# One row of W_down per partition, loaded from ScalarE's queue in transfers of 95 and 33 partitions

## The chip, the cores and the metric

The kernel runs on one core of one Trainium2 chip. The core has five engines that run side by side and wait for each other on semaphores: TensorE (PE in the profile) for matrix products, VectorE (DVE), ScalarE (ACT), GpSimd (POOL) and SyncE (SP). Data comes from the chip's memory into the on-chip buffer through 16 DMA engines. A load is issued by one of the engines into its own queue; the DMA engines then move it, packet by packet, and count a semaphore up as they finish. The metric is the time of one execution in device microseconds (us). Lower is better.

## The reference

One decode step, four sequences (B = 4), one token each, model width D = 576, in bfloat16:

```python
x = A_x
h = x + _A_ref(_layernorm(x), A_k_cache, A_v_cache, A_wq, A_wo)
h2 = h + _B_ref(_layernorm(h), B_W_gate, B_W_up, B_W_down)
```

`_A_ref` is attention with 32 query heads and 16 key/value heads of 128 over the last 4096 positions of a cache of 16384, with a softmax, followed by the product with `wo` (4096 x 576). `_B_ref` is a gated feed-forward layer:

```python
gate = x @ W_gate                    # 576 -> 4608
up   = x @ W_up                      # 576 -> 4608
h    = gate * (gate > 0) * up
return h @ W_down                    # 4608 -> 576
```

With one token per sequence nearly all of the work is reading: 159.6 MB of cache and weights are used once each.

## The kernel before

**Stages.** The kernel goes through `wq` and the queries, then through 16 groups of four key/value heads (each loads 4 MB of keys and 4 MB of values), then `wo`, then the gate and up products, then the product with W_down, and stores 4 x 576 values.

**Where loads land.** One large buffer, `pool`, has four slots of 4 MB. Keys and values go round these slots; `wo`, W_gate, W_up and W_down take the same space when its former users are done. `transfers` is the list of all loads in order, and SyncE issues them in that order (`prog_sync`), each after the instructions that last used its space.

**W_down.** It is laid out with 36 rows per partition: partition p holds rows 36p to 36p + 35, each of 576 values (1152 bytes), one after the other. `WD` at line 253 cuts the 36 rows of every partition into six pieces, (0, 14), (14, 23), (23, 29), (29, 33), (33, 35) and (35, 36), and each piece is one transfer of 128 partitions with its own semaphore (`wd0` to `wd5`). All six wait for "ATTN", the last product with `wo`, as they overwrite it. They are the last loads of the program.

**The end of the program, by engine.** ScalarE (`prog_act`, lines 345 to 358): after the attention it copies `oX`, takes the root for the second layer norm, copies the transposed activations (N1, N2), makes `hn4` in two activations (line 353, HN40 and HN41), then for each of three column ranges (`CUTS`) applies a relu to the gate product when PE has it (line 356), and at last casts the first 320 output columns. VectorE multiplies the up product by that (line 449), transposes the result in two halves (line 453, HHT 0 and 1), and casts the other output columns. PE (`prog_pe`) does the gate and up products (lines 573 to 592; each of the two is read in a part of four rows and a rest, with a semaphore each), and then, at lines 594 to 603, goes through the pieces of W_down in order: it waits for the piece's landing, and for the transposed half that it needs, and does two matmuls for each of the piece's rows.

**Names.** `S.op` and `S.dma` put an instruction on an engine's list, with the names that it waits for (`deps`) and the name under which others wait for it. `land(name)` is the name of a transfer's landing. On each engine the instructions run in the order in which they were put there. All matmuls are recorded at lines 466 and 468 of a helper, so the profile shows them under these lines and under the names of their tiles: `val<-pool,probT` at the end of the program is the product with W_down.

Of the kernel before, what the change touches and what calls it, by code (L numbers as in the profile page):

```python
# [12 lines left out]
D = 576  # L13
# [24 lines left out]
JJ = 36  # L38
# [63 lines left out]
def bass_sequential_preLN__sliding_block_cached__glu_gated_reglu__decode_kernel(  # L102
# [12 lines left out]
    with ExitStack() as es:  # L115
        cnt = [0]

        def sb(name, shape, dt):
            return es.enter_context(nc.sbuf_tensor(name, shape, dt))

        pool = sb("pool", [128, NSLOT * QUAD], BF16)
# [66 lines left out]
        def part(u, k, order):  # L188
            f0, f1 = CUTS[k]
            return pb[GUB[u][k]][:, 0:(f1 - f0) * JJ].rearrange("p (f j) -> p " + order, j=JJ)  # L190

        def down(u):
            n0, n1 = OUTS[u]
            return pb[DNB][32 * u:32 * u + B, 0:n1 - n0]
        tpv = pb[TPB].bitcast(BF16)

        S = Sched()
# [3 lines left out]
        transfers = []  # L201
# [49 lines left out]

        wd_sb = pool[:, 0:FC * D].rearrange("p (j n) -> p j n", j=JJ)
        WD = [(0, 14), (14, 23), (23, 29), (29, 33), (33, 35), (35, 36)]
        for k, (f0, f1) in enumerate(WD):
            transfers.append((("wd", k), f"wd{k}", ["ATTN"],
                              lambda e, f0=f0, f1=f1: e.dma_start(
                                  out=pool[:, f0 * D:f1 * D], in_=B_W_down.rearrange("(p j) n -> p (j n)", j=JJ)[:, f0 * D:f1 * D])))

        def feat(c):
            return slice(c, c + 509, 4) if c < 4 else slice(512, D)  # L260
# [1 line left out]
        def land(name):  # L262
            return ("L",) + (name if isinstance(name, tuple) else (name,))
# [25 lines left out]
        def prog_act(S):  # L289
# [3 lines left out]
                 deps=["D_VAR", "EPS"], name="A_STD")  # L293
            S.op(a, lambda e: e.copy(out=dup[:, :].rearrange("p (r u) -> p r u", u=2),
                                     in_=bass.AP(tensor=ident_b, offset=0, ap=[[128, 64], [1, 64], [0, 2]])), deps=["IDB"], name="DUP")
            S.op(a, lambda e: e.copy(out=col[:, :].rearrange("p (a s) -> p a s", s=NS),
                                     in_=bass.AP(tensor=ident_b, offset=0, ap=[[128, NS], [0, 128], [1, NS]])), name="COL")
# [3 lines left out]
                                           in_=bass.AP(tensor=ident_b, offset=0, ap=[[128, NS], [0, 16], [1, NS], [0, 2]]),  # L301
# [4 lines left out]
                                     in_=bass.AP(tensor=mask, offset=0, ap=[[NHQ, 128], [0, 16], [1, NHQ]])), deps=["M0"], name="SAME")  # L306
            for u in range(2):
                S.op(a, lambda e, u=u: e.activation(out=xn4[:, u, 0:B], in_=pb[STB][:, 0:B], func=ACT.Copy, scale=par[:, u:u + 1]),
                     deps=["XDUP", "PAR2", "XN4Z"], name=f"XN4{u}")
            for k in range(2):  # L310
                S.op(a, lambda e, k=k: e.copy(out=q_bf[:, k, :].rearrange("p (x e k) -> p x e k", e=2, k=32),
                                              in_=pb[QB[k]].rearrange("p (x k e) -> p x e k", e=2, k=32)), deps=["QMM"], name=f"QBF{k}")
            S.op(a, lambda e: e.copy(out=qrep[:, :, :].rearrange("p x (g y) -> p x g y", g=4),
                                     in_=sc.ap().rearrange("p (g r) -> p g r", g=4)[:, :, 0:128].rearrange("p g (x y) -> p x g y", x=4)),
                 deps=["QREP"], name="D_QR")
# [16 lines left out]
            for i in range(NQUAD):  # L332
                S.op(a, lambda e, i=i: e.activation(out=diag[:, i % 2, :], in_=spot[:, :], func=ACT.Copy, scale=rmx[:, i % 2:i % 2 + 1]),  # L333
                     deps=[("RMAX", i), "SPOT"], name=("DIAG", i))
                deps = [("BIAS", i)]
                if i >= 2:
                    deps.append(("TRP", i - 2))
                S.op(a, lambda e, i=i: e.activation(  # L338
                    out=Pb[:, (i % 2) * 1024:(i % 2 + 1) * 1024], in_=sc[:, (i % 2) * 1024:(i % 2 + 1) * 1024], func=ACT.Exp,
                    scale=SCALE, bias=bias[:, i % 2:i % 2 + 1], accum_out=rs1[:, i:i + 1]),  # L340
                    deps=deps, name=("EXP", i))
                if i + 2 < NQUAD:
                    qzero(i + 2)
            S.op(a, lambda e: e.copy(out=bass.AP(tensor=spread, offset=0, ap=[[16 * H, H], [4 * H + 1, 4], [4, H]]),
                                     in_=bass.AP(tensor=ident_b, offset=0, ap=[[128, H], [0, 4], [1, H]])),
                 deps=["SP0"], name="SPREAD")
            S.op(a, lambda e: e.copy(out=oX[:, :, :].rearrange("p e b -> p (e b)"), in_=pb[0][:, 0:EO * B]), deps=["OSEL"], name="OX")  # L347
            S.op(a, lambda e: e.activation(out=st2[:, 14:15], in_=st2[:, 13:14], func=ACT.Sqrt, bias=eps_c[0:B, 0:1], scale=1.0),
                 deps=["D_VAR2"], name="A_STD2")
            S.op(a, lambda e: e.copy(out=hnT[0:64, 4, 0:B], in_=tpv[0:64, 16:20]), deps=["TP2", "HN4Z"], name="N1")  # L350
            S.op(a, lambda e: e.copy(out=hnT[:, 0:4, 0:B], in_=tpv[:, 0:16].rearrange("p (c b) -> p c b", b=B)), name="N2")
            for u in range(2):
                S.op(a, lambda e, u=u: e.activation(out=hn4[:, u, 0:B], in_=pb[SUB][:, 400:400 + B], func=ACT.Copy, scale=par[:, u:u + 1]),
                     deps=["HDUP"], name=f"HN4{u}")
            for k, (f0, f1) in enumerate(CUTS):
                S.op(a, lambda e, k=k, f0=f0, f1=f1: e.activation(out=gate_sb[:, :, f0:f1].rearrange("p j f -> p f j"), in_=part(0, k, "f j"), func=ACT.Relu),
                     deps=[("GATE", k)], name=("RELU", k))
# [101 lines left out]
        def prog_pe(S):  # L459
            t = "tensor"  # L460

            def mm(o, l, r, start, stop, deps=(), name=None, skip=False, held=False):

                def make(e):
                    if not held:
                        return e.matmul(o, lhsT=l, rhs=r, start=start, stop=stop, skip_group_check=skip)  # L466
                    tile = tuple(next(x for x in (32, 64, 128) if x >= n) for n in (l.shape[0], l.shape[-1]))
                    return e.add_instruction(mybir.InstMatmult(  # L468
                        name=nc.get_next_instruction_name(), start_tensor_calc=start, stop_tensor_calc=stop, bass_skip_group_check=skip,
                        tile_size=tile, tile_position=(0, o.offset // o.ap[0][0] % 128), ldweights=False,  # L470
                        ins=[e.lower_ap(r), e.lower_ap(l)], outs=[e.lower_ap(o)]))

                S.op(t, make, deps=deps, name=name, signal=name is not None)
# [9 lines left out]
            for c in (4, 0, 1, 2, 3):  # L483
                s = at[("wq", 0)] + c * HQ if c < 4 else at[("wq", 4)]
                deps = [land(("wq", 0)), "D_XNT"] if c == 0 else [land(("wq", 4)), "XN41"] if c == 4 else []
                for g in range(4):
                    x0 = s + (g if c < 4 else g % 2) * 1024
                    for k in range(2):
                        mm(pb[QB[k]][32 * g:32 * g + 32, :], xnT[:, c, :] if c < 4 else xn4[:, g // 2, :], pool[:, x0 + 512 * k:x0 + 512 * k + 512], c == 4, c == 3,
                           deps=deps, name="QMM" if c == 3 and g == 3 and k == 1 else None, skip=True, held=k == 1)  # L490
                        deps = []
            for g in range(4):
                mm(pb[g][:, 0:128].rearrange("p (x h b) -> p x h b", x=4, b=B), sel[32 * g:32 * g + 32, :, :].rearrange("p g k -> p (g k)"),
                   qT[32 * g:32 * g + 32, :].rearrange("p (h x b) -> p x h b", x=4, b=32)[:, :, :, 0:B], True, True,
                   deps=["D_QT", "SEL"] if g == 0 else [], name="QREP" if g == 3 else None)
# [42 lines left out]
            for i in range(NQUAD + VLEAD):  # L538
# [5 lines left out]
                if i >= VLEAD:  # L544
                    j = i - VLEAD
# [7 lines left out]
            for q in range(4):  # L553
                mm(pb[0][:, 0:EO * B], spread[:, q, :, :].rearrange("p h k -> p (h k)"), o_bf[:, q * EO:(q + 1) * EO, :].rearrange("p e b -> p (e b)"), q == 0, q == 3,
                   deps=["NORM", "SPREAD"] if q == 0 else [], name="OSEL" if q == 3 else None)
            for e_ in range(EO):
                deps = [land(("wo",)), "OX"] if e_ == 0 else []
                for u in range(2):
                    c0 = at[("wo",)] + e_ * D + u * HD
                    mm(attn[:, u * HD:(u + 1) * HD], oX[:, e_, :], pool[:, c0:c0 + HD], e_ == 0, e_ == EO - 1,  # L560
                       deps=deps, name="ATTN" if e_ == EO - 1 and u == 1 else None, held=u == 1)
                    deps = []
# [10 lines left out]
            for u, kind in ((0, "wg"), (1, "wu")):  # L573
                if u == 1:
                    residual()
                for c in range(4):
                    s = at[(kind, 0)] + c * F
                    deps = [land((kind, 0))] + (["N2"] if c == 0 and u == 0 else [])
                    for k, (f0, f1) in enumerate(CUTS):
                        for q in range(4):  # L580
# [3 lines left out]
                            deps = []  # L584
                s = at[(kind, 4)]
                deps = [land((kind, 4)), "HN41"]
                for k, (f0, f1) in enumerate(CUTS):
                    for q in range(4):
                        x0 = s + (q % 2) * FQ
                        mm(pb[GUB[u][k]][32 * q:32 * q + 32, 0:(f1 - f0) * JJ], hn4[:, q // 2, :], pool[:, x0 + f0 * JJ:x0 + f1 * JJ],  # L590
                           False, True, deps=deps, name=(("GATE", "GU")[u], k) if q == 3 else None, skip=True, held=k > 0)
                        deps = []

            for k, (f0, f1) in enumerate(WD):
                deps = [land(("wd", k))]
                for f in range(f0, f1):
                    if f % (JJ // 2) == 0:
                        deps = deps + [("HHT", f // (JJ // 2))]
                    for u in range(2):
                        last = f == FC - 1  # L600
                        mm(down(u), hhT[:, f, 0:B], wd_sb[:, f, OUTS[u][0]:OUTS[u][1]], False, last,
                           deps=deps, name="DOWN1" if last and u == 1 else None, skip=True)
                        deps = []

        progs = [("gpsimd", prog_pool), ("sync", prog_sync), ("scalar", prog_act), ("vector", prog_dve), ("tensor", prog_pe)]
        S.begin(False)
        for _, p in progs:
# [32 lines left out]
```

## Time and profile before

| what | value |
|---|---|
| median of 3 runs | 377.72 us (377.6 to 378.23) |
| the profiled execution | 378.56 us, of which the span from first to last instruction is 377.2 us |
| read from memory | 159.58 MB, 423 GB/s over the span |
| SyncE's queue (q1) | 6488 packets, 98.8% of 16 engines' span |
| instruction loads (q8) | 8 packets, 0.13 MB |
| the six W_down transfers | 2016, 1296, 864, 576, 288 and 144 KB; 15.0, 17.7, 19.3, 20.2, 20.4 and 20.3 us from issue to landing |
| mean granted TensorE clock | 0.923 |

How to read it: times are counted from the start of the span. In the timeline a line gives the start, the duration, the engine, the line of the kernel, the operation, what it writes and reads, how many instructions were merged, and in square brackets how long the engine was idle before and what ended that. PEld is PE's loading of weights. In tables by stretch of time, the columns are the stretch, its length, the busy time and number of instructions of PE, PEld, DVE, ACT and POOL, the granted clock, the mean busy share of the 16 DMA engines, and GB/s; a packet is counted where it starts, so a share can come out a little over 1. Section 3 of the page gives for each queue its packets, megabytes and the time that its packets took as a share of all 16 engines. The trace doesn't say which of the 16 engines moved a packet.

### The profile page before, as it was taken

Reading aid. Unit: us, or ns where it says so; the run is one execution under the profiler, and the core shown is the slowest. Engines: PE = TensorE matmul, PEld = TensorE weight load, DVE = VectorE, ACT = ScalarE, POOL = GpSimd, SP = SyncE. Lnnn points to the kernel's source line nnn. Section 1 sums busy time; section 2 is a strip of 40 time slices with the busy share of each in tenths; the row PEclk is TensorE's granted clock in tenths of the full one; section 3 lists DMA queues with packets and bytes.
Section 4 is the critical chain, followed back from the end, with each engine's and each line's share of the span. In section 5 each row is a group of like instructions: output and inputs, shape, how many; then the busy total and the mean of one; then the engine's idle time right before and its main releaser. Section 6 shows DMA issues by size and latency. Waiting matters only on the chain.

```text
span 377.2 us, 2603 instructions
## 1 busy us (share of the span) xinstructions
PE 302.2 (80%) x1432; PEld 73.0 (19%) x772; DVE 225.8 (60%) x165; ACT 53.4 (14%) x140; POOL 5.2 (1%) x15
## 2 busy tenths in 40 slices
PE   0509299969996999499969996899879996968667
PEld 0101022212221222022212221122112121212214
DVE  8046677595849493858476846666675768231230
ACT  2202402110220112002200220020202010101020
POOL 5000000000000000000000000000000000000000
PEclk9999789998999899989989997799959998996988
DMA  8999999999999999999999999999999999999996
GB/s 334 445 445 389 445 440 393 445 440 438 422 424 441 438 434 408 441 441 427 413 440 441 431 427 427 440 434 427 420 441 440 417 424 441 422 432 429 443 404 255
DMA packets 6506, 159.74 MB, mean 423 GB/s; under 512 B 728, under 2 KB 864, under 8 KB 1632
## 3 DMA queue, kind: packets, MB, share of 16 engines
q1 hardware_dynamic: 6488, 159.59, 98.8%
q8 instruction: 8, 0.13, 0.1%
q10 hardware_dynamic: 8, 0.00, 0.0%
q14 instruction: 2, 0.02, 0.0%
HBM read 159.58 MB, written 0.00 MB: 423 GB/s over the span
## 4 chain that ended last, share of the span: by engine, by line
DMA 47%; DVE 29%; PE 20%; ACT 3%; SPq 1%; issue 1%; DVEq 0%
DMA pool<-in_A_k_cache_dram 41%; DVE kT L403 20%; PE sc L466 7%; PE sc L468 6%; DMA pool<-in_B_W_down_dram 5%; DVE acc L420 4%; PE val L466 3%; PE val L468 3%; DVE own_sb L417 2%; DVE probT L414 2%; ACT P L338 2%; PE pb L466 1%; DVE o_bf L442 0%; ACT L338 0%; DVE rmx L406 0%
## 5 line engine op out<-in xcount | busy, mean ns | idle before, releaser
L403 DVE STREAM_TRANSPOSE kT<-pool 128x2048 f32<-128x2048 f32 x64 | 142.8, 2278 | 25.3 <-DMA pool<-in_A_k_cache_dram 24.3
L466 PE MATMUL sc<-kT,qz 128*128 128x512 bf16 x256 | 110.5, 432 | 36.6 <-DVE kT L403 36.3
L468 PE MATMUL sc<-kT,qz 128*128 128x512 bf16 x256 | 109.6, 428 | 0.0
L466 PE MATMUL val<-pool,probT 128*64 128x512 bf16 (+2 forms) x328 | 104.2, 374 | 4.4 <-DMA pool<-in_B_W_down_dram 4.4
L468 PE MATMUL val<-pool,probT 128*64 128x512 bf16 x256 | 96.2, 379 | 0.0
L466 PEld LDWEIGHTS sc<-kT,qz 128*128 128x128 bf16 x256 | 26.7, 104 | 146.5 <-issue 71.1
L466 PEld LDWEIGHTS val<-pool,probT 128*64 128x64 bf16 (+1 forms) x328 | 32.1, 107 | 81.3 <-issue 68.5
L406 DVE TENSOR_REDUCE rmx<-sc 128x1 f32<-128x1024 f32 x16 | 19.6, 1225 | 41.0 <-PE sc L468 41.0
L333 ACT ACTIVATE diag<-spot,rmx 128x16 f32<-128x16 f32 x16 | 4.9, 307 | 234.0 <-DVE rmx L406 234.0
L414 DVE STREAM_TRANSPOSE probT<-P 128x1024 bf16<-128x1024 bf16 x16 | 19.9, 1246 | 21.0 <-ACT P L338 21.0
L338 ACT ACTIVATE P<-sc,bias 128x1024 bf16<-128x1024 f32 x16 | 17.8, 1114 | 21.0 <-DVE bias L409 21.0
L327 ACT COPY qz<-qrep 32x128 bf16<-32x128 bf16 x64 | 18.8, 294 | 0.6
L409 DVE TENSOR_REDUCE bias<-pb 128x1 f32<-128x16 f32 x16 | 2.8, 175 | 23.8 <-PE pb L466 23.8
L420 DVE TENSOR_REDUCE acc<-own_sb 128x128 f32<-128x1024 f32 x8 | 15.2, 1897 | 0.3
L417 DVE TENSOR_TENSOR own_sb<-val,mask 128x1024 f32<-128x1024 f32 x8 | 9.6, 1200 | 7.9 <-PE val L468 7.9
L466 PE MATMUL sc<-pool,oX 128*4 128x288 bf16 x32 | 10.0, 338 | 0.4 <-ACT oX L347 0.4
L468 PE MATMUL sc<-pool,oX 128*4 128x288 bf16 x32 | 9.9, 336 | 0.0
L478 PE MATMUL pb<-ident_b,xn_bf 4*128 4x4 bf16 (+1 forms) x5 | 0.4, 180 | 10.0 <-DVE xn_bf L371 10.0
L466 PE MATMUL sc<-qT,sel 32*128 32x128 bf16 x4 | 0.3, 284 | 9.6 <-DVE qT L427 9.6
L445 DVE TENSOR_TENSOR h_row<-sc,x_bf 4x576 f32<-4x576 f32 x1 | 0.7, 745 | 11.6 <-PE sc L468 11.6
L466 PE MATMUL pb<-diag,same 128*128 128x16 f32 x32 | 6.3, 273 | 1.7 <-ACT diag L333 1.7
L466 PEld LDWEIGHTS pb<-diag,same 128*128 128x128 f32 x32 | 4.8, 188 | 11.8 <-ACT diag L333 7.4
(102 smaller groups left out, 85.7 us busy)
## 6 DMA issues: line engine op xcount, KB each, us to landing
pool<-in_A_k_cache_dram SPq DMA_DIRECT2D x16, 4096.0 KB, 26.8
pool<-in_A_v_cache_dram SPq DMA_DIRECT2D x16, 4096.0 KB, 26.4
pool<-in_A_wo_dram SPq DMA_DIRECT2D x1, 4608.0 KB, 18.3
pool<-in_B_W_gate_dram SPq DMA_DIRECT2D x1, 4608.0 KB, 18.6
pool<-in_B_W_up_dram SPq DMA_DIRECT2D x1, 4608.0 KB, 24.7
pool<-in_A_wq_dram SPq DMA_DIRECT2D x1, 4096.0 KB, 12.7
pool<-in_B_W_down_dram SPq DMA_DIRECT2D x1, 2016.0 KB, 15.0
pool<-in_B_W_down_dram SPq DMA_DIRECT2D x1, 1296.0 KB, 17.7
```

The lines of the kernel that those rows point to most:

```text
L327: S.op(a, lambda e, src=src, dst=dst: e.copy(out=dst, in_=src), deps=deps, name=("QZ", i) if g == 3 else None, signal=g == 3)
L333: S.op(a, lambda e, i=i: e.activation(out=diag[:, i % 2, :], in_=spot[:, :], func=ACT.Copy, scale=rmx[:, i % 2:i % 2 + 1]), deps=[("RMAX", ...
L338: S.op(a, lambda e, i=i: e.activation(out=Pb[:, (i % 2) * 1024:(i % 2 + 1) * 1024], in_=sc[:, (i % 2) * 1024:(i % 2 + 1) * 1024], func=ACT ...
L403: S.op(v, lambda e: e.transpose(out=dst, in_=src), deps=deps, name=("TR", f))
L406: S.op(v, lambda e: e.tensor_reduce(out=rmx[:, i % 2:i % 2 + 1], in_=sc[:, (i % 2) * 1024:(i % 2 + 1) * 1024], axis=AX.X, op=ALU.max), dep ...
L409: S.op(v, lambda e: e.tensor_reduce(out=bias[:, i % 2:i % 2 + 1], in_=pb[TPB][:, 16 * (i % 2):16 * (i % 2) + 16], axis=AX.X, op=ALU.min), ...
L414: S.op(v, lambda e: e.transpose(out=pT[i % NPT], in_=Pb[:, (i % 2) * 1024:(i % 2 + 1) * 1024]), deps=[("EXP", i)] + ([("PV", i - NPT)] if ...
L417: S.op(v, lambda e: e.tensor_tensor(out=own_sb[:, :].rearrange("p (x d) -> p x d", d=DH), in0=val[:, :].rearrange("p (x d) -> p x d", d=DH ...
L420: S.op(v, lambda e: e.tensor_reduce(out=acc[:, w % 2, :], in_=own_sb[:, :].rearrange("p (x d) -> p d x", d=DH), axis=AX.X, op=ALU.add), de ...
L445: S.op(v, lambda e: e.tensor_tensor(out=h_row[:, :], in0=attn, in1=x_bf[:, :], op=ALU.add), deps=["ATTN", land("x")], name="H")
L466: return e.matmul(o, lhsT=l, rhs=r, start=start, stop=stop, skip_group_check=skip)
L468: return e.add_instruction(mybir.InstMatmult(name=nc.get_next_instruction_name(), start_tensor_calc=start, stop_tensor_calc=stop, bass_ski ...
```

## The change

Row 28 of every partition, the last of piece 2, is left out of SyncE's third W_down transfer, which so has 5 rows per partition in place of 6. It is loaded by two further transfers, one for partitions 0 to 94 and one for partitions 95 to 127. ScalarE issues them, behind the `hn4` activations and in front of the first gate activation; they wait for ATTN, and they share one semaphore, `wdrow`, whose full count is named by the second. PE waits for that count, besides `wd2`, in front of piece 2. The bytes loaded, the place where they land and all arithmetic are the same.

```diff
         WD = [(0, 14), (14, 23), (23, 29), (29, 33), (33, 35), (35, 36)]
+        wd_src = B_W_down.rearrange("(p j) n -> p (j n)", j=JJ)
+
+        def piece(f0, f1, p0=0, p1=128):
+            return lambda e: e.dma_start(out=pool[p0:p1, f0 * D:f1 * D], in_=wd_src[p0:p1, f0 * D:f1 * D])
+
         for k, (f0, f1) in enumerate(WD):
-            transfers.append((("wd", k), f"wd{k}", ["ATTN"],
-                              lambda e, f0=f0, f1=f1: e.dma_start(
-                                  out=pool[:, f0 * D:f1 * D], in_=B_W_down.rearrange("(p j) n -> p (j n)", j=JJ)[:, f0 * D:f1 * D])))
+            transfers.append((("wd", k), f"wd{k}", ["ATTN"], piece(f0, f1 - (k == 2))))
...
                      deps=["HDUP"], name=f"HN4{u}")
+            for p0, p1 in ((0, 95), (95, 128)):
+                S.dma("scalar", piece(28, 29, p0, p1), "wdrow", deps=["ATTN"], name=land("wdrow") if p0 else None)
             for k, (f0, f1) in enumerate(CUTS):
...
             for k, (f0, f1) in enumerate(WD):
-                deps = [land(("wd", k))]
+                deps = [land(("wd", k))] + ([land("wdrow")] if k == 2 else [])
                 for f in range(f0, f1):
```

## The prediction

> **What bounds the kernel now.** I read the page first: how much the transfers fill the span, and what closes the chain.
>
> ```profile
> span 377.2 us, 2603 instructions
> PE 302.2 (80%) x1432; PEld 73.0 (19%) x772; DVE 225.8 (60%) x165; ACT 53.4 (14%) x140; POOL 5.2 (1%) x15
> DMA packets 6506, 159.74 MB, mean 423 GB/s; under 512 B 728, under 2 KB 864, under 8 KB 1632
> q1 hardware_dynamic: 6488, 159.59, 98.8%
> q8 instruction: 8, 0.13, 0.1%
> q10 hardware_dynamic: 8, 0.00, 0.0%
> ```
>
> SyncE's queue (q1) keeps the 16 DMA engines busy for 98.8% of the span. Nothing on PE, DVE or ACT can shorten that; only fewer bytes, a shorter start or a shorter end can. So I read the end: the chain of waits in order of time, then the timeline of PE and ACT.
>
> ```profile
> 353.78 20.18 DMA pool<-in_B_W_down_dram
> 374.00 0.70 PE val L466 x7
> 374.72 0.68 PE val L466 x5
> 375.42 0.42 DVE out_sb L456
> ```
> ```profile
> 356.32 0.42 ACT L353 ACTIVATE hn<-val,par 128x4 bf16<-128x4 f32 x2 [0.20 <-PE val L466]
> 359.76 1.51 ACT L356 ACTIVATE P<-sc 128x396 f32<-128x396 f32 x2 [3.02 <-PE sc L466]
> 361.07 0.10 PEld L466 LDWEIGHTS pb<-pool,hnT 128*32 128x32 bf16 x4 [0.71 <-DMA pool<-in_B_W_up_dram]
> 367.48 4.95 PE L466 MATMUL val<-pool,probT 128*4 128x320 bf16 x46 [3.77 <-DMA pool<-in_B_W_down_dram]
> 372.63 0.98 PE L466 MATMUL val<-pool,probT 128*4 128x320 bf16 x12 [0.21 <-DMA pool<-in_B_W_down_dram]
> 375.07 0.08 PEld L466 LDWEIGHTS val<-pool,probT 128*4 128x4 bf16 x2 [0.27 <-DMA pool<-in_B_W_down_dram]
> ```
>
> From 353.78 on the end is set by W_down's landings: PE waits before the pieces wd0, wd2, wd3, wd4 and wd5, and behind the last landing only two matmuls, two casts and the store are left. So the last engine's last row is the end. Do the 16 engines stop together? Short windows of the tail show it (the last two columns are the DMA share and GB/s):
>
> ```profile
> 372.40:372.80 0.40, 0.19 (x5) 0.15 (x6) 0.00 (x0) 0.00 (x0) 0.00 (x0) 1.00 1.03 400
> 373.00:373.20 0.20, 0.20 (x9) 0.18 (x4) 0.00 (x0) 0.00 (x0) 0.00 (x0) 1.00 0.61 242
> 373.60:373.80 0.20, 0.01 (x1) 0.00 (x0) 0.00 (x0) 0.00 (x0) 0.00 (x0) 1.00 0.51 202
> 374.00:374.20 0.20, 0.20 (x4) 0.17 (x6) 0.00 (x0) 0.00 (x0) 0.00 (x0) 1.00 0.51 184
> 374.40:374.60 0.20, 0.20 (x5) 0.00 (x0) 0.00 (x0) 0.00 (x0) 0.00 (x0) 1.00 0.08 29
> ```
>
> They don't. Between 372.8 and 373.1 the share falls from 1.03 to 0.61: six engines have stopped. It holds at 0.51, eight engines, until 374.2, and at 374.5 about one is left (0.08). So eight engines run some 1.5 us behind the best, and one of them a further 0.2 to 0.3 us. The page fits: eight instruction loads of 16 KB (q8: 8 packets, 0.13 MB), each about 1 us on one engine, and eight late engines. The trace doesn't number the engines, and this is what the prediction turns on.
>
> **The change, part by part.** The sum is made against the profiled execution, 378.56 us with a span of 377.2; the median of the runs is 377.72, and I add the difference to the median.
>
> *ScalarE issues two transfers in front of gate's activations.* The one issue on ScalarE, x's, took 554 ns, so two take 1.1 us. They stand behind the hn activations (done at 356.74) and in front of the first gate activation, which waits 3.02 us for PE until 359.76. They end near 357.9: 1.9 us of cover. Were it gone, the gate activations, DVE's products and its transposes would slip by at most 1.1 us; the transposes end at 366.4 and PE waits for wd0 until 367.48, so that too would cost almost nothing. The wait on ATTN ends at 352.4, before ScalarE gets there. Cost 0.
>
> *SyncE keeps its 45 loads.* The third piece of W_down has 5 rows per partition in place of 6; an issue there is the same instruction. Cost 0.
>
> *PE waits for one more landing, wdrow, in front of piece 2.* Queued behind it are 26 matmuls, the casts and the store. PE reaches that point at 372.43, some 14.5 us after the second issue. SyncE's transfers issued at 352 to 355 took 15.0 to 20.4 us to land because they queue behind each other; the new rows stand in ScalarE's queue. If that queue takes turns row by row, each engine has about 26 SyncE rows to serve before wd1 is in (2 of W_up's long ones, then 8 each of three transfers) against at most 22 new ones, so wdrow lands in time. Cost 0; what it costs if not is in rival two.
>
> *The same bytes on other engines.* Each 128-row load makes 128 data packets and 16 completions (45 x 144 + 8 = 6488 in q1); x with 4 rows makes 4 and 4 (q10: 8). So 128 rows go as 8 to each of 16 engines, 4 rows as 1 to each of 4: equal shares. Equal shares of 95 = 5 x 19 on at most 16 engines are 19 rows on 5; of 33 = 3 x 11, 3 rows on 11. The other end is an even spread, about 8 rows each, which changes nothing. I take equal shares, since both rows of the trace have them. [...]
>
> *Price of a row.* With all engines busy (369.0 to 369.6: 438 GB/s at a share of 1.038) an engine moves 422 / 16 = 26.4 bytes per ns. Between 374.10 and 374.25, 24 packets, 22 of them of 1152 B, kept 54.5% of 16 engines busy: 1.308 us, less two of 2304 B at 87 ns, is 52 ns each. Between 374.0 and 374.7, 28.0% for 54 such rows, 3 of 2304 B and 11 completions leaves 6 ns for a completion. Inside a longer row, 1152 B cost 44 ns, so taking row 28 out of piece 2 saves each engine 8 x 44 = 350 ns. Then:
> - engines in the five: 19 x 52 + 6 - 350 = +640 ns, and +810 ns if they also take 3 of the 33;
> - engines with 3 rows only: 3 x 52 + 6 - 350 = -190 ns;
> - engines with none: -350 ns.
>
> *Rows that alternate with another queue's.* Not in this trace for such rows. Below: the two 8 KB loads of q14 at 78 us took 1.5% of 16 x 2.5 us, 0.3 us each, which is their bytes at 26.4 B/ns: nothing extra. Above: a 16 KB load of q8 took 1.5% of 16 x 4 us = 0.96 us at 56 us and 1.12 us at 360, against 0.62 by bytes: 0.34 to 0.50 extra for one change of queue. A gain is excluded, as the engines are full. I take nothing extra (8 KB is nearer to 1152 B) and keep the other end for the range.
>
> *The sum.* The end moves with the latest engine. If at least one of the five is among the eight late ones, the end is that engine's: +0.64 to +0.81 if it is the very last, 0.25 less if it is one of the other seven: +0.4 to +0.8, and I take 0.65. If all five are early, the latest lose 0.19 to 0.35: that much gain. Which? Five fixed engines miss eight late ones only if the eight lie in the other eleven: 4 of 16 placings if the eight are neighbours on a ring, 165 of 12870 if they are scattered. So the likelier is a loss: 377.72 + 0.65 = 378.4 us.
>
> **The rivals.**
> *One: the five are the early ones.* Six engines stop by 373.1, so five with 1.5 us to spare exist; with +0.81 they end near 373.9, still before the others. The end comes 0.19 to 0.35 earlier, 377.4 to 377.5; PE's own work allows it (it is free at 372.43, 373.61 and before each later piece). Against it: the placing count above. It is the case on the other side of no change.
>
> *Two: a change of queue costs.* At 0.42 us each, once per transfer: 2 x 0.42 + 0.81 = +1.65, 379.4. Once per row on the five: 22 x 0.42 + 0.81 = +10.05, 387.8, and PE would then wait for wdrow itself. From some 5 ns per row on it lifts the forecast over the 0.2% line. For it: all eight q8 loads go with late engines. Against: q14's two.
>
> *Three: spread evenly.* Then the same rows run on the same engines at 52 in place of 44 ns: 8 x 8 ns = +0.06 us, 377.8. [...]
>
> **How the numbers follow.** 0.2% is 0.755 us, about what a measurement of this kernel can tell from no change. Forecast (late engines loaded): 0.40; its prices run from +0.4 to +0.8 with nothing added for the change of queue and a few ns per row carry it over the line, so I put 0.22 of it above and 0.18 within. Queue change: 0.30, slower. Early five: 0.18, within. Even: 0.07, within. Something that gains more than 0.755, as engines lagging less for a reason not seen: 0.05. Together slower 0.52, same 0.43, faster 0.05. The range reaches down to 377.3 (early five) and up to 380.5, past one change per transfer; it leaves out the per-row end (about 0.10) and the larger gain. The forecast's own range is 378.1 to 378.7.
>
> **What would show it.** Equal shares: q10 with 8 + 128 + 5 + 11 = 152 packets; evenly spread, 8 + 128 + 32 = 168. Right: a tail in which fewer engines work longer, with a DMA share near 0.31 (five engines) or less after 374.6, and PE's last wait ending at 375.5 to 375.9 in place of 375.07. Early five: the plateau at 0.51 ends 0.2 to 0.35 sooner and PE's last wait ends at 374.7 to 374.9. Queue change: q10's share above its 128 x 52 ns = 6.7 us (0.1% of 16 engines' span), or PE's wait in front of piece 2 grown. ScalarE's first gate activation moved would show the issue not covered. I am wrong if the last landing doesn't move, or if a PE wait other than W_down's takes the end.

## The result, and the profile after

| | median (us) | executions | lowest to highest |
|---|---|---|---|
| before | 377.75 | 17 | 377.56 to 378.42 |
| after | 378.57 | 17 | 378.15 to 379.1 |

After over before is 1.0019, 95% interval [1.0013, 1.0026]: 0.8 us slower. The forecast was 378.4 us, in the range 377.3 to 380.5. The total came out near it. The way to the total did not.

The two profiled executions have nearly the same time (378.56 before, 378.61 after; spans 377.2 and 377.3), so their spans must not be compared directly: in the profiled execution of after, the loads ahead of the change, which it doesn't touch, ran about 0.8 us earlier. I take a mark ahead of the change, the packet with which the first DMA engine completes the last part of W_gate. From there to the last completion of W_down it was 347.87 to 374.69 before, 26.82 us, and 347.06 to 374.69 after, 27.63 us. The tail is 0.81 us longer, as the medians are.

The page of after, its span and its DMA lines (queue: packets, MB, share of 16 engines' span):

```profile
span 377.3 us, 2606 instructions
DMA packets 6650, 159.74 MB, mean 423 GB/s; under 512 B 744, under 2 KB 1008, under 8 KB 1776
q1 hardware_dynamic: 6488, 159.44, 98.7%
q8 instruction: 8, 0.13, 0.1%
q10 hardware_dynamic: 152, 0.15, 0.1%
```

q10 has 152 packets: 8 for x, 128 rows, and 5 + 11 completions. That is the equal-shares case; an even spread would have made 168.

The end of the chain of waits of after, in order of time (start, duration, what; its pieces of 0.02 to 0.04 us called "issue" are left out):

```profile
351.01 23.00 DMA pool<-in_B_W_down_dram
374.05 0.71 PE val L471 x7
374.77 0.66 PE val L471 x5
375.46 0.42 DVE out_sb L461
```

It is the same chain as before: W_down's landings set the end, and behind them only the last matmuls and the casts are left. The timeline of after, for ScalarE's first gate activation and for PE's waits:

```profile
357.43 1.49 ACT L361 ACTIVATE P<-sc 128x396 f32<-128x396 f32 x2 [3.45 <-PE sc L471]
360.71 0.11 PEld L471 LDWEIGHTS pb<-pool,hnT 128*32 128x32 bf16 x4 [3.00 <-DMA pool<-in_B_W_up_dram]
367.77 4.56 PE L471 MATMUL val<-pool,probT 128*4 128x320 bf16 x46 [3.05 <-DMA pool<-in_B_W_down_dram]
372.67 0.98 PE L471 MATMUL val<-pool,probT 128*4 128x320 bf16 x12 [0.33 <-DMA pool<-in_B_W_down_dram]
374.05 1.36 PE L471 MATMUL val<-pool,probT 128*4 128x320 bf16 x14 [0.41 <-DMA pool<-in_B_W_down_dram]
375.11 0.08 PEld L471 LDWEIGHTS val<-pool,probT 128*4 128x4 bf16 x2 [0.25 <-DMA pool<-in_B_W_down_dram]
```

The gate activation waited for PE, 3.45 us, and not for the two issues ahead of it. No wait in front of piece 2 takes the end: the last of the new rows was complete at 368.9, two us ahead of piece 1. PE's last wait ends at 375.11, against 375.07 before; counted from the mark that is 28.05 us against 27.20. So the last landing did move, by about 0.85 us, a little past the 0.43 to 0.83 that the prediction named as its sign.

The short windows of the tail of after (the last two columns are the DMA share and GB/s):

```profile
372.40:372.80 0.40, 0.13 (x3) 0.11 (x5) 0.00 (x0) 0.00 (x0) 0.00 (x0) 1.00 0.92 369
373.00:373.20 0.20, 0.20 (x7) 0.19 (x4) 0.00 (x0) 0.00 (x0) 0.00 (x0) 1.00 0.72 271
373.60:373.80 0.20, 0.04 (x1) 0.00 (x0) 0.00 (x0) 0.00 (x0) 0.00 (x0) 1.00 0.64 248
374.00:374.20 0.20, 0.15 (x4) 0.13 (x6) 0.00 (x0) 0.00 (x0) 0.00 (x0) 1.00 0.55 196
374.40:374.60 0.20, 0.20 (x6) 0.01 (x1) 0.00 (x0) 0.00 (x0) 0.00 (x0) 1.00 0.10 35
```

The staircase is still there. But these windows stand at the times of before's page, and after's loads run 0.81 us ahead of them. Moved by that much, before's windows of 373.6 and 374.6 are these two of after:

```profile
372.79:372.99 0.20, 0.20 (x6) 0.20 (x4) 0.00 (x0) 0.00 (x0) 0.00 (x0) 1.00 0.79 323
373.79:373.99 0.20, 0.00 (x0) 0.00 (x0) 0.00 (x0) 0.00 (x0) 0.00 (x0) 1.00 0.64 230
```

The share is 0.79 where before had 0.51, and 0.64, ten engines, where the prediction's sign was 0.31 or less, five engines or fewer. So not a few engines work longer, but most of them.

Where did the time come from? The answer lies ahead of the tail, in the stretch in which the new rows run. The DMA view of 358.5 to 368.5 us, before:

```profile
DMA packets 428, 4.04 MB, mean 404 GB/s; under 512 B 54, under 2 KB 54, under 8 KB 190
q1 hardware_dynamic: 427, 4.03, 95.6%
q8 instruction: 1, 0.02, 0.7%
```

and after:

```profile
DMA packets 507, 3.70 MB, mean 370 GB/s; under 512 B 60, under 2 KB 168, under 8 KB 287
q1 hardware_dynamic: 384, 3.57, 91.5%
q10 hardware_dynamic: 123, 0.12, 4.0%
```

The engines are as busy as before: 96.3% of 16 x 10 us then, 95.5% now. They move less. Before, 4.04 MB in 154.1 us of engine time is 26.2 bytes per ns; after, 3.70 MB in 152.8 us is 24.2. The new rows themselves aren't the reason: q10's 4.0% is 6.4 us for 108 rows of 57 ns and 15 completions of 9, where the forecast had 52 ns for a row. It is SyncE's rows that took longer: 91.5% for 3.57 MB is 24.4 bytes per ns, and for the 16128-byte rows of piece 0 the mean went from 607 to 644 ns. At 24.2 in place of 26.2 each engine loses 7.6% of 9.55 us, 0.73 us, also the five engines that carry none of the new rows.

I use this number, the bytes that a busy engine moves per ns between 358.5 and 368.5 us, as the measure in all the runs below: MB of the stretch over the summed shares times 160 us. A loss per engine follows as above, against 26.2.

### The profile page after: what moved, and what is told of

Read it like the earlier page. It is cut to its first block, busy times and chain, and to the rows that moved or that the text cites. A ratio compares the mean times of both kernels' runs of the same rounds, so it can differ in the third digit from the quotient of the medians.

```text
span 377.3 us, 2606 instructions
## 1 busy us (share of the span) xinstructions
PE 300.0 (80%) x1432; PEld 72.7 (19%) x772; DVE 225.8 (60%) x165; ACT 53.4 (14%) x140; POOL 5.2 (1%) x15
## 3 DMA queue, kind: packets, MB, share of 16 engines
q1 hardware_dynamic: 6488, 159.44, 98.7%
## 4 chain that ended last, share of the span: by engine, by line
DMA 47%; DVE 31%; PE 18%; ACT 3%; SPq 1%; issue 1%; DVEq 0%
DMA pool<-in_A_k_cache_dram 41%; DVE kT L408 21%; DMA pool<-in_B_W_down_dram 6%; PE sc L471 6%; PE sc L473 5%; DVE acc L425 4%; PE val L471 3%; PE val L473 3%; DVE own_sb L422 2%; DVE probT L419 2%; ACT P L341 2%; PE pb L471 1%; DVE o_bf L447 0%; ACT L341 0%; DVE rmx L411 0%
## 5 line engine op out<-in xcount | busy, mean ns | idle before, releaser
L408 DVE STREAM_TRANSPOSE kT<-pool 128x2048 f32<-128x2048 f32 x64 | 142.8, 2278 | 26.3 <-DMA pool<-in_A_k_cache_dram 25.5
L471 PE MATMUL sc<-kT,qz 128*128 128x512 bf16 x256 | 109.2, 426 | 36.9 <-DVE kT L408 36.6
L473 PE MATMUL sc<-kT,qz 128*128 128x512 bf16 x256 | 108.2, 423 | 0.0
L471 PEld LDWEIGHTS sc<-kT,qz 128*128 128x128 bf16 x256 | 26.4, 103 | 145.4 <-DVE kT L408 70.6
L471 PE MATMUL sc<-pool,oX 128*4 128x288 bf16 x32 | 9.0, 314 | 0.4 <-ACT oX L350 0.4
L473 PE MATMUL sc<-pool,oX 128*4 128x288 bf16 x32 | 9.0, 314 | 0.0
## 6 DMA issues: line engine op xcount, KB each, us to landing
pool<-in_A_v_cache_dram SPq DMA_DIRECT2D x16, 4096.0 KB, 26.4
```

Of the source, the lines that this page charges most:

```text
L408: S.op(v, lambda e: e.transpose(out=dst, in_=src), deps=deps, name=("TR", f))
L473: return e.add_instruction(mybir.InstMatmult(name=nc.get_next_instruction_name(), start_tensor_calc=start, stop_tensor_calc=stop, bass_ski ...
```

## The experiments

Theory A is the forecast's: five engines with 19 rows end later. Theory B: rows that are written to partitions which their engine doesn't serve in a 128-partition load slow the other rows. Theory C: any second queue does it. No trace shows which partitions an engine serves in such a load; but a load of 128 rows has 16 completions (q1: 6488 packets, 45 x 144 + 8), 8 rows to an engine by equal shares, so of the 22 rows that each of five engines carries in after at least 14 are not among those.

### One row of 128 partitions, and 96 + 32

```diff
-            for p0, p1 in ((0, 95), (95, 128)):
-                S.dma("scalar", piece(28, 29, p0, p1), "wdrow", deps=["ATTN"], name=land("wdrow") if p0 else None)
+            for p0, p1 in ((0, 128),):
+                S.dma("scalar", piece(28, 29, p0, p1), "wdrow", deps=["ATTN"], name=land("wdrow"))
```

> Row 28 as one transfer of 128 partitions, from ScalarE's queue at the same place. Theory A (prediction: 19 and 3 rows heaped on five and six engines, of which some stop late): the heap is gone, 377.8 us, +0.05. Theory B (the traces of before and after: in the ten us in which the extra rows run, all engines are as busy but move 387 GB/s in place of 420, so rows that engines write outside their usual partitions slow everybody): the engines write their usual partitions, 377.8, and the rate stays near 420 per full share. Theory C (any second queue beside SyncE's slows the rows): +0.6 to +0.8, 378.4, rate near 390.

Measured: 377.95 us, before 377.78, ratio 1.0001 [0.9993, 1.001]. The DMA view of 358.5 to 368.5 us of this run:

```profile
DMA packets 572, 4.19 MB, mean 419 GB/s; under 512 B 69, under 2 KB 197, under 8 KB 334
q1 hardware_dynamic: 427, 4.02, 95.4%
q8 instruction: 1, 0.02, 0.7%
q10 hardware_dynamic: 144, 0.15, 4.3%
```

144 packets from the second queue in that stretch, and 4.19 MB in 160.6 us is 26.1 bytes per ns, as before. A second queue costs nothing here. C falls, and with it the price per change of queue. The rows are the same 128 as in after, from the same place to the same place; only the number of transfers, and which engine carries which row, are different.

```diff
-            for p0, p1 in ((0, 95), (95, 128)):
+            for p0, p1 in ((0, 96), (96, 128)):
```

> [...] q10 has 8 + 128 + 32 = 168 packets. A (heap): 377.8, +0.05 to +0.1. B (other partitions): +0.4 to +0.8, 378.1 to 378.5, rate near 390 per full share while they run. C (second queue): +0.6 to +0.8.

Measured: 378.24 us, ratio 1.001 [1.0001, 1.0019]. q10 has 168 packets, so both transfers go to all 16 engines, 6 and 2 rows each, and there are no five engines with more. It still lost: 3.86 MB in 153.1 us is 25.2 bytes per ns, 0.37 us per engine. A has nothing to offer for that; B has, if the engines carry other partitions here than in a load of 128, which no trace shows.

### The same two transfers from SyncE's queue

```diff
+            if k == 2:
+                transfers.append(("wdrow_a", "wdrow", ["ATTN"], piece(28, 29, 0, 95)))
+                transfers.append(("wdrow", "wdrow", ["ATTN"], piece(28, 29, 95, 128)))
...
-            for p0, p1 in ((0, 95), (95, 128)):
-                S.dma("scalar", piece(28, 29, p0, p1), "wdrow", deps=["ATTN"], name=land("wdrow") if p0 else None)
```

> The same 95 and 33 partitions, issued by SyncE in front of its third W_down transfer; ScalarE issues nothing. A (heap): as the changed kernel, 378.4 to 378.6. B (other partitions): as the changed kernel, 378.3 to 378.6, with the lower rate near 369 to 372 us, where the rows now stand. C (second queue): the slowing is gone and only the heap is left, 378.0 to 378.2.

Measured: 378.43 us, ratio 1.0018 [1.001, 1.0027], the same loss as after's. The rows now come later, and in 361 to 371 us 24.2 bytes per ns move (3.88 MB at 100.4%), where before has 26.4 (4.18 MB at 99.1%): 0.84 us per engine. So it is the shape of the transfers, whichever queue they are in.

### Two rows of W_down in place of one

```diff
-            transfers.append((("wd", k), f"wd{k}", ["ATTN"], piece(f0, f1 - (k == 2))))
+            transfers.append((("wd", k), f"wd{k}", ["ATTN"], piece(f0, f1 - 2 * (k == 2))))
...
-                S.dma("scalar", piece(28, 29, p0, p1), "wdrow", deps=["ATTN"], name=land("wdrow") if p0 else None)
+                S.dma("scalar", piece(27, 29, p0, p1), "wdrow", deps=["ATTN"], name=land("wdrow") if p0 else None)
```

> Rows 27 and 28 of every partition, 2304 B, in the two transfers of 95 and 33 from ScalarE; SyncE's third transfer has 4. Twice the bytes, as many packets. A (heap): five engines get 19 + 3 rows of about 90 to 100 ns and lose 700: +1.3 to +1.5 on those, 379.0 to 379.3. B (bytes outside the usual partitions slow everybody): twice the loss in rate, +1.4 to +1.7, 379.2 to 379.5. C (second queue, by packets): as one row, 378.5.

Measured: 379.68 us (5 executions), ratio 1.0049 [1.0035, 1.0062]: +1.9 us by the medians, a little over twice after's loss. That is more than A (+1.3 to +1.5) and B (+1.4 to +1.7) expected, and far from C's 378.5; the run doesn't choose between A and B. 22.5 bytes per ns; the 16128-byte rows took 693 ns. The loss grows with the bytes that are moved in this shape.

### Row 28 not loaded

```diff
-            for p0, p1 in ((0, 95), (95, 128)):
-                S.dma("scalar", piece(28, 29, p0, p1), "wdrow", deps=["ATTN"], name=land("wdrow") if p0 else None)
```

PE's wait for these rows goes too.

> Row 28 isn't loaded at all (its product uses what stood there): SyncE's third transfer has 5 rows, ScalarE issues nothing. It prices the row itself. Both theories: -350 ns on every engine, 377.4 us, ratio 0.9991; less if PE, which is free only 0.16 us before that piece's landing, holds the end.

Measured: 377.52 us, before 377.81, ratio 0.9993 [0.9984, 1.0002]: -0.27 us, where the sum had -0.35 for a row less on each engine. 26.2 bytes per ns. The interval holds no change as well, but the trace shows the term: from the mark to its end an engine takes 24.50 to 24.55 us, where before has 24.84 to 24.88, 0.33 us less (the one engine that an instruction load hits in that stretch is left out in both).

### 64 + 64

```diff
-            for p0, p1 in ((0, 95), (95, 128)):
+            for p0, p1 in ((0, 64), (64, 128)):
```

> Row 28 as partitions 0 to 63 and 64 to 127 from ScalarE, 4 + 4 rows to each engine. A (heap): 377.8, as the single transfer. [...]

Measured: 378.57 us, ratio 1.0017 [1.0008, 1.0026]. A's 377.8 is missed. By equal shares each engine carries 4 + 4 rows, as many as it had, and the loss is as large as with 95 + 33: 24.3 bytes per ns, 0.70 us per engine.

### Five rows at a time, at two sets of partitions

Here the rows of W_down stay where they were. Three transfers of five rows of 5760 bytes are added, into space that nothing uses, so that by equal shares five engines carry three rows each (q10 has 38 packets: 8 for x, 15 rows and 15 completions, five to a transfer). Only the partitions differ: 0, 4, 8, 12, 16 in the first run, 64, 68, 72, 76, 80 in the second, each time also the ones 1 and 2 beyond. In these runs and in those below, PE waits for the added rows in front of the last piece.

```diff
+            src = B_W_down.rearrange("(p j) n -> p (j n)", j=JJ)
+            for r in range(3):
+                q = 0 + r        # second run: 64 + r
+                S.dma("scalar", lambda e, q=q: e.dma_start(out=pool[q:q + 17:4, FC * D:FC * D + 2880], in_=src[q:q + 17:4, 0:2880]),
+                      "extra", deps=["ATTN"], name=land("extra") if r == 2 else None)
...
-                deps = [land(("wd", k))]
+                deps = [land(("wd", k))] + ([land("extra")] if k == 5 else [])
```

> [...] 15 rows of 220 ns, 0.66 us on each of five engines. A (heap): as these five stop 0.9 us or more before the last, +0 to +0.2. [...]

> [...] A (heap): as own5, +0 to +0.2. [...]

Measured: 377.89 us, 0.9998 [0.9989, 1.0007], with partitions 0 to 18; 378.73 us, 1.0019 [1.001, 1.0028], with 64 to 82. The DMA view of 358.5 to 368.5 us, partitions 0 to 18:

```profile
DMA packets 458, 4.19 MB, mean 419 GB/s; under 512 B 64, under 2 KB 64, under 8 KB 213
q1 hardware_dynamic: 427, 4.09, 97.1%
q10 hardware_dynamic: 30, 0.09, 2.2%
q8 instruction: 1, 0.02, 0.6%
```

and partitions 64 to 82:

```profile
DMA packets 425, 3.88 MB, mean 388 GB/s; under 512 B 63, under 2 KB 63, under 8 KB 206
q1 hardware_dynamic: 394, 3.77, 96.3%
q10 hardware_dynamic: 30, 0.09, 2.4%
q8 instruction: 1, 0.02, 0.7%
```

The two have the same number of rows, bytes and packets. 26.2 bytes per ns in the one, 24.4 in the other, 0.68 us per engine. A expected +0 to +0.2 us in both: the first run fits, the second doesn't. This is the plainest pair of the study: which partitions the rows go to decides. A row's place in memory goes with its partition in all these runs, so they don't tell whether the writing or the reading is what costs. The first run also shows that three transfers in a second queue, as such, cost nothing (0.9998). In the second it is not only the engines with the rows that lose: the eleven engines that carry no extra row kept their distances to each other and all came some 0.7 us later, 25.5 to 25.6 us from the mark to their end in place of 24.8 to 24.9 (again without the one that an instruction load hits).

A's 0.9 us takes these five engines for the five of the 95 rows; no run shows whether they are, nor which engines have partitions 0 to 18 and 64 to 82 in a load of 128.

### Partitions shifted by four, and 17 rows on one engine

Two further theories, on rows that go to other partitions than those their engine serves in a load of 128. Theory O: such a row costs only the engine that serves its partition there. Theory G: all engines lose while it is written. The five-row transfers again, shifted by four partitions:

```diff
-                q = 0 + r
+                q = 4 + r
```

> The run with three transfers of five rows to partitions 0, 4, 8, 12, 16 (and 1 and 2 beyond each), shifted by four partitions: 4, 8, 12, 16, 20. [...] Theory G (all engines lose while rows are written out of place): the same loss as with partitions 64 to 80, +0.7 us, 378.4 to 378.6. If only a row to the other half of the partitions costs something: no change, 377.8.

and one transfer of 17 rows, which one engine carries; with 8 rows to an engine in a load of 128, at least 9 of the 17 are such rows:

```diff
+            src = B_W_down.rearrange("(p j) n -> p (j n)", j=JJ)
+            S.dma("scalar", lambda e: e.dma_start(out=pool[0:17, FC * D:FC * D + D], in_=src[0:17, 0:D]),
+                  "extra", deps=["ATTN"], name=land("extra"))
```

> The kernel before, with one extra transfer of 17 partitions (0 to 16), 1152 B each, from ScalarE's queue in front of gate's activations into unused space. [...]

Measured: the shift gives 378.55 us, 1.0016 [1.0007, 1.0025]; four partitions are enough. Twelve of its 15 rows are also in the run with partitions 0 to 18, from the same place to the same place, and cost nothing there; that other engines carry them now is the author's estimate, from shares taken in order of the partitions, and no trace shows it. Its view of 358.5 to 368.5 us:

```profile
DMA packets 440, 4.01 MB, mean 401 GB/s; under 512 B 65, under 2 KB 65, under 8 KB 209
q1 hardware_dynamic: 410, 3.91, 96.6%
q10 hardware_dynamic: 29, 0.08, 2.3%
q8 instruction: 1, 0.02, 0.8%
```

25.1 bytes per ns, 0.42 us per engine. Seven 36864-byte rows of W_up that started between 358.73 and 358.94 took 258 to 343 ns longer than the median of 1368: many engines stood at the same time, not one after the other. That is theory G.

The 17 rows give 377.89 us, 0.9998 [0.9989, 1.0007], and 26.1 bytes per ns. They went out on one engine (q10 has 26 packets: 8 for x, 17 rows, one completion), one at a time, nearly all 0.43 to 0.45 or 0.64 to 0.66 us apart, for 8 us. That is theory O. The runs contradict each other if either theory is to hold for every such row.

### One row at a time, at two sets of partitions

The two differ in the size of the rows and in how many engines write at once. So: five transfers of one row of 5760 bytes each, once to partitions 0 to 3 and 32, once to 64 to 67 and 96. The author took the first set as in place and the second as out of place, and one engine for all five rows; no trace here shows either (q10 has 18 packets: 8 for x, five rows, five completions).

```diff
+            src = B_W_down.rearrange("(p j) n -> p (j n)", j=JJ)
+            for r in range(5):
+                q = 0 + (r if r < 4 else 32)     # second run: 64 + ...
+                S.dma("scalar", lambda e, q=q: e.dma_start(out=pool[q:q + 1, FC * D:FC * D + 2880], in_=src[q:q + 1, 0:2880]),
+                      "extra", deps=["ATTN"], name=land("extra") if r == 4 else None)
```

> [...] One row makes one share, so one engine carries all five rows one after the other: 5 x 220 ns = 1.1 us of its own. Both theories expect no loss of the other engines; the one engine ends 1.1 us later than before, which shows only if it starts among the last: 377.8 to 378.2, and the stretch from W_gate's rest landing to the last W_down row as long as before but for that engine.

> The same five transfers by the same engine, to partitions 64, 65, 66, 67 and 96. Theory Bytes (what is lost goes by the bytes that are written out of place, by all engines alike): a third of the run with 15 rows to partitions 64 to 80, which cost each engine 0.7 us: +0.23 us on all engines, 378.0 to 378.4. Theory Together (engines lose only where several rows are written out of place at the same time): no loss of the other engines, the same time as with the five rows in place, within 0.1 us in the trace.

Measured: 377.8 us, 1.0 [0.9991, 1.0009], with partitions 0 to 3 and 32; 377.79 us, 0.9996 [0.9987, 1.0005], with 64 to 67 and 96. The view of 358.5 to 368.5 us of the second:

```profile
DMA packets 441, 4.11 MB, mean 411 GB/s; under 512 B 52, under 2 KB 52, under 8 KB 191
q1 hardware_dynamic: 430, 4.06, 97.4%
q10 hardware_dynamic: 10, 0.03, 0.7%
q8 instruction: 1, 0.02, 0.7%
```

26.0 bytes per ns, 0.08 us per engine, against 26.2 in the first. Summed over the packets of the queue, the five rows of the second lengthened the other rows by 1.4 us, about 1.3 times the 1.1 us that they took themselves. The theory by bytes wanted 0.23 us per engine, 3.7 us in all. For 15 rows on five engines at once it was 10.6 us to partitions 64 and beyond and 6.2 us with the shift, 3.2 and 1.9 times the 3.3 us of those rows. So neither theory holds to the letter: these rows in transfers of one cost the others 1.3 times their own time, too little to move the end, and in transfers of five 1.9 and 3.2 times, shared out over all engines. It goes more with Together than with Bytes.

### All runs in one table

| run | median (us) | over before | bytes per ns of a busy engine | lost per engine (us) |
|---|---|---|---|---|
| before | 377.8 | | 26.2 | |
| after, 95 + 33 | 378.57 | 1.0019 | 24.2 | 0.73 |
| 95 + 33 from SyncE | 378.43 | 1.0018 | 24.2 (before there 26.4) | 0.84 |
| two rows, 95 + 33 | 379.68 | 1.0049 | 22.5 | 1.37 (the rows go on to 372) |
| 64 + 64 | 378.57 | 1.0017 | 24.3 | 0.70 |
| 96 + 32 | 378.24 | 1.001 | 25.2 | 0.37 |
| 128 | 377.95 | 1.0001 | 26.1 | 0.04 |
| row 28 left out | 377.52 | 0.9993 | 26.2 | 0 |
| 5 rows x 3, partitions 0 to 18 | 377.89 | 0.9998 | 26.2 | 0 |
| 5 rows x 3, partitions 64 to 82 | 378.73 | 1.0019 | 24.4 | 0.68 |
| 5 rows x 3, partitions 4 to 22 | 378.55 | 1.0016 | 25.1 | 0.42 |
| 17 rows on one engine | 377.89 | 0.9998 | 26.1 | 0.04 |
| 1 row x 5, partitions 0 to 3, 32 | 377.8 | 1.0 | 26.2 | 0 |
| 1 row x 5, partitions 64 to 67, 96 | 377.79 | 0.9996 | 26.0 | 0.08 |

No version here is shown to be faster than before: 377.52 us goes with a part of W_down left out, and its interval holds no change.

## Why the prediction came out near, and where it was wrong

**The issues, SyncE's loads and PE's extra wait: right.** All cost nothing, as the timeline above shows. An issue took 0.27 and 0.34 us on ScalarE's side, less than the 554 ns counted.

**Equal shares: right.** 152 packets, and following each engine's packets through the trace (its next starts where its last ended) gives five engines with 22 rows, six with 3 and five with none.

**The price of a row: right.** 52.3 ns in the run with 128 partitions (56.5 in after, where all rows are slowed); the row taken out of piece 2 is worth 0.33 us on each engine by the run without it, against 0.35.

**"If at least one of the five is among the eight late ones": this did not happen.** In the profiled execution of after the five engines stood, at the mark ahead of the change, 0.05, 0.07, 0.15, 1.12 and 1.26 us behind the first one; none of the eight late ones is among them (seven of those stood 1.6 to 1.9 us behind, and an instruction load at 358.2 made the eighth). At the end they are 0.96, 0.96, 1.04, 2.02 and 2.17 behind, and the late group ends at 1.59 to 1.75. So the last engine is one of the five, one that was neither early nor late, and it is 0.42 us behind the late group. With nothing but its own rows, +0.81, it would have ended at 2.07 behind the old first engine, where before's last one ended at 1.96: hardly slower than before. Rival one would have been nearly right then, without its gain. That last one of before is the engine that took the last instruction load, at 360.45: it stood only 0.42 behind at the mark, and its stretch is 26.41 us where the others have 24.84 to 24.88. So which engine is the very last hangs on where that load falls, which the sum didn't ask.

**"Nothing extra for rows that alternate with another queue's": this is the term that failed.** It was bounded by prices of a change of queue, and that was the wrong thing to price. A change of queue costs nothing (128 rows in one transfer from ScalarE: 1.0001). Equal shares of 95 and 33 do something else that the sum left out: they move rows to engines that don't serve those partitions in the 128-row loads (22 rows on each of five engines, where such a load gives it 8). The runs of this shape lost 0.7 to 0.8 us on every engine. A 3-row engine shows it best: forecast at -0.19, the first one's stretch from the mark to its end went from 24.86 to 25.46 us, +0.60, so 0.79 was lost.

**The sum again, with that term.** The last of the five stood 1.26 us behind at the mark. Its 22 rows, less the row saved in piece 2, add 0.81 and the shared loss 0.79, together 2.86 us. On top of the old first engine's 24.86 us that makes 27.7; the trace has 27.63. Before's last was at 26.82. The forecast of +0.65 was near +0.82 by luck: a lateness that wasn't there and a loss that wasn't counted were of like size.

**The rivals.** Two (a change of queue) has the right sign of a loss and the wrong cause. Three, the even spread, was worked out at +0.06 us for the same rows on the same engines; the one transfer of 128 is that case, and its 1.0001 fits. 96 + 32 and 64 + 64 are spread evenly too, but in two transfers, and measured about +0.4 and +0.7.

**What stays open.** Why all engines wait when rows of these shapes are in flight, and why the cost differs (0.70 us per engine with 64 + 64 and 0.37 with 96 + 32, 0.68 with partitions 64 to 82 and 0.42 with 4 to 22). These runs also differ in what the rows ran beside: those of 96 + 32 went out at 358.0 to 361.8 us and those of 64 + 64 at 360.6 to 367.7, more of them beside rows of 16128 bytes; those to partitions 4 to 22 at 358.5 to 361.4 and those to 64 to 82 at 359.4 to 363.8. No run separates that from the shape. Which engines stand at fault can't be read, as the trace doesn't number them. No run shows where the rows wait, nor whether it is in the reading or in the writing.

## What to carry to other kernels

Where the DMA engines are the bound, it is worth asking what a load in other shapes than 128 partitions costs: 96 + 32, 64 + 64 and 95 + 33 of the same bytes cost 0.1 to 0.2% here, one transfer of 128 nothing. When engines are fully busy, look at the bytes that a busy engine moves, not only at the share: here the stalls showed as longer packets (644 ns in place of 607) and not as idle time. And a total that comes out right should still be taken apart: here two errors covered for each other.

## What the runs showed of the hardware that was not expected

- Three transfers of five rows are free at partitions 0 to 18 (0.9998) and cost 0.16% at 4 to 22 and 0.19% at 64 to 82.
- The loss falls also on engines that carry no such row: some 0.7 us on each of eleven with partitions 64 to 82.
- Fewer rows at a time cost hardly anything: 0.04 us per engine for 17 rows of 1152 bytes on one engine, 0.08 us for five transfers of one row of 5760.
- Rows of two queues on one engine took turns one by one: 15 of the 16 steps from one of the 17 rows to the next were as long as one row of 16128 or 10368 bytes of SyncE's queue, about 0.65 or 0.44 us, and this alone cost nothing (0.9998).
